# Block-sparse attention and a Fourier mixing layer on one core: head pair 6 without mask matmuls, fewer first transfers, last turn by DMA, a new written order

## Chip, core and metric

The kernel runs on one NeuronCore of a Trainium2 chip. The metric is the device time of one execution in microseconds, as the median of several runs. Five engines work side by side, each through its own instructions in order: PE (TensorE: matmuls and transposes, which write PSUM), DVE (VectorE), ACT (ScalarE), POOL (GpSimd) and SP (SyncE, which here only issues DMA transfers). They wait for each other by semaphores. An engine whose next instruction must wait does nothing else in the meantime.

## What is computed

Attention over 4 batches, 8 heads, 768 positions, head size 64. A query sees the keys of its own block of 64 and of the best blocks out of 12, by the score of the query with each block's mean key, all under the causal mask:

```python
k_rep = k.reshape(B, H, 12, 64, D).mean(axis=3)
gate = where(causal_blocks, einsum('bhsd,bhnd->bhsn', q, k_rep), -1e9)
sel = top 3 of gate for each query, and its own block
scores = where(sel & causal, q @ k.T / sqrt(D), -1e9)
x = softmax(scores) @ v                    # to (4, 768, 512)
X = fft(fft(x, axis=1), axis=2)
u = x + real(X)
un = (u - mean(u)) / sqrt(var(u) + 1e-6)
out = u + relu(un @ w_ch1) @ w_ch2         # 512 -> 2048 -> 512
```

## The kernel before

Work goes by *head pair*: two heads of one batch, 16 pairs in all, pair P in batch P // 4. The order of all work is written out by hand in `ORDER` (L117): a list of some thousand steps such as `s:6,1` (score tile 1 of pair 6). The loop at its end calls one small function for each, and every engine runs its instructions in the order in which they are issued there. The steps that matter here:

- Loads: `Lk`, `Lq`, `Lv` bring a pair's k, q and v in through SP's queue, `LT` and `LF` the two Fourier tables (`fs_sb`, `fd_sb`), `Lc` further constants, among them 0/1 block rows (`ind`) for the score operands; `W:0` to `W:2` bring w_ch1 in three chunks through POOL's queue, for hidden tiles 0-3, 4-9 and 10-15.
- Attention of a pair: `tk`, `tq` turn k and q on PE (six fp32 transposes each, L293). `ks` (DVE, L298) sums k by blocks, `kh` multiplies by a 0/1 table `half` to keep the two heads apart, `qc` (DVE, L317) copies q, `kc` (ACT) and `qs` (POOL) write k and q as fp16 score operands into one of three slots `qk_s`. `g` (PE) is the gate, `gt`, `gx`, `gl`, `gm` (DVE) find the third largest and make a mask of 0 and a large negative number, turned back. `s:P,i` (PE) are the scores of tile i out of 6, `e` (ACT, L432) the exponentials, `d` (POOL, L438) clears what is above the diagonal, `vc` (POOL) casts v, `v` (PE, L450) is the product with v, `x` (DVE) divides.
- Masks come in two forms. Pairs under `NX` = 7 add the mask to the scores by extra matmuls (L422): a block table times the mask, four for each piece of a tile. From pair 7 on, the mask stands as 32 further rows (64 to 95) beside the 64 rows of q, and the block rows beside those of k, so that one matmul with 96 rows does both (L415); step `K` (POOL, L229) writes these rows with 8 copies. In this form each head has a plane of its own in the slot, and q and k are written as two half copies. Pairs of the first form use one plane of a slot, chosen by `XW`.
- Fourier layer of a batch: `fs`, `fd`, `f` (DVE) fold x by symmetry; `y:b,h` (PE, L519) transforms along the features; for the row at the middle frequency, three one-column matmuls (L525) are added twice a batch. `tr` (DVE) and `ty` (ACT) copy it out, `m` (PE, L553, L554) transforms along positions, `u` (DVE, L567) adds x and sums, `xu` (ACT, L579) centres.
- Turn of the centred rows to put the features on partitions: for batches 0 and 3 by PE transposes (`xt`, L586) and a DVE copy (`un`, L591), for batches 1 and 2 by DMA transposes on SP's queue (`un`, L594).
- Hidden layer: `w:b,it` (PE, L630 and L632) makes hidden tile `it` of 16, `r` (ACT L642, every fourth DVE L640) the relu, `c:b,st,h` (PE, L649) multiplies row tile `st` of 6 with w_ch2 over half h of the hidden tiles, `o` (DVE, L655) scales and adds u, `od` (SP, L660) writes out. `bn`, `nv`, `nr` make the variance and its root.

`u` tiles live in five buffers, three a batch, so a later `u` waits until an earlier one was written out. PSUM is handed out as four buffers to every PE product. At the start 12 matmuls on zeros (`warmps`, L677) run while the first k and q arrive; the identity for the transposes (`id32`) and `half` are loaded by DMA on ACT's queue.

Of the kernel before, what the change touches and what calls it, by code (L numbers as in the profile page):

```python
# [20 lines left out]
DM = 512  # L21
# [7 lines left out]
def _consts_np():  # L29
# [36 lines left out]
    for e in range(2):  # L66
        ind[e, 16 * e:16 * e + NB] = nn[:, None] == (s[None, :] // 64)
    half = np.zeros((128, 2, NB), np.float32)
    half[0:64, 0] = 1.0
    half[64:128, 1] = 1.0  # L70
    return dict(FS=fs.astype(np.float16), FD=fd.astype(np.float16),
                ident32=np.eye(128, dtype=np.float32),
# [4 lines left out]
                ind=ind.transpose(1, 0, 2).copy().astype(np.float16),  # L77
                half=half.reshape(128, 24))
# [39 lines left out]
Lk:1 Lq:1 Lk:2 tk:0 tq:0 Lk:3 Lq:2 ks:0 Lq:3 qc:0 tk:1 iz:1 kh:0 qs:0 g:0 ks:1 iz:0 gt:0 kc:0 tq:1  # L118
kh:1 gx:0 kc:1 Lq:4 Lk:4 Lv:0 gl:0,0 tk:2 gl:0,1 gm:0 qc:1 kc:2 s:0,1 s:0,0 ks:2 e:0,1 qs:1 g:1
e:0,0 gt:1 s:0,2 s:0,3 gx:1 e:0,2 tq:2 gl:1,0 tk:3 e:0,3 kh:2 Lq:5 Lv:1 Lk:5 gl:1,1 qc:2 s:0,5  # L120
d:0,3 s:0,4 e:0,5 gm:1 d:0,2 tq:3 ks:3 e:0,4 d:0,5 qs:2 g:2 qc:3 kc:3 d:0,4 s:1,0 gt:2 qs:3 s:1,5
e:1,0 s:1,2 gx:2 tq:4 d:0,0 e:1,5 kh:3 gl:2,0 e:1,2 s:1,1 gl:2,1 s:1,3 qc:4 e:1,1 tk:4 vc:0 gm:2
e:1,3 g:3 ks:4 d:0,1 Lv:2 Lq:6 d:1,5 s:1,4 gt:3 d:1,1 tq:5 e:1,4 d:1,3 gx:3 qs:4 v:0 kc:4 qc:5
d:1,2 d:1,0 d:1,4 s:2,5 x:0 s:2,0 vc:1 e:2,5 s:2,1 e:2,0 s:2,4 d:2,5 Lv:3 Lk:6 Lq:7 LT:0 gl:3,0
v:1 e:2,1 fs:0,0 gl:3,1 kh:4 gm:3 e:2,4 d:2,1 s:2,2 x:1 d:2,0 g:4 vc:2 e:2,2 s:3,2 gt:4 Lv:4 s:2,3
fs:1,0 e:3,2 fs:1,1 tk:5 Lc:0 LF:0 Lq:8 Lk:7 qs:5 gx:4 e:2,3 Lk:8 s:3,4 ks:5 d:3,2 tq:6 d:2,4
e:3,4 fs:0,1 gl:4,0 s:3,1 Lq:9 kh:5 kc:5 gl:4,1 g:5 d:3,4 qc:6 d:2,2 e:3,1 d:2,3 s:3,0 gm:4 vc:3
tk:6 e:3,0 gt:5 d:3,1 s:3,5 Lv:5 Lk:9 ks:6 s:3,3 e:3,5 v:2 e:3,3 d:3,5 gx:5 d:3,0 kh:6 gl:5,0 kc:6
d:3,3 s:4,5 x:2 s:4,2 qs:6 e:4,5 s:4,1 e:4,2 v:3 gl:5,1 fs:2,1 e:4,1 gm:5 d:4,2 fs:2,0 s:5,5 x:3
s:5,4 e:5,5 s:5,1 e:5,4 d:5,5 g:6 fd:2,0 e:5,1 fs:3,0 s:5,2 fs:3,1 s:5,0 fd:2,1 e:5,2 fd:3,1 s:5,3  # L130
fd:3,0 e:5,0 gt:6 s:4,0 f:0,1 s:4,3 e:5,3 f:0,0 s:4,4 gx:6 e:4,0 y:0,0 f:0,3 e:4,3 gl:6,0 f:0,2
e:4,4 gl:6,1 y:0,1 pg:0 tr:0,0 d:5,0 d:4,5 d:4,3 gm:6 tk:7 ty:0,0 d:4,4 tr:0,1 d:5,1 tq:8 d:5,3
vc:4 ks:7 ty:0,1 m:0,2 W:0 qc:8 Lv:6 kc:7 tk:8 d:4,0 u:0,2 d:4,1 tq:7 W:1 kc:8 m:0,0 Lq:10 Lk:10
qc:7 d:5,4 vc:5 m:0,1 u:0,0 xu:0,2 d:5,2 Lv:7 Lq:11 Lk:11 v:4 qs:7 ks:8 xu:0,0 s:6,5 u:0,1 s:6,0
W:2 e:6,5 e:6,0 s:6,3 qs:8 x:4 xt:0,0 xu:0,1 xt:0,2 un:0,0 tq:9 e:6,3 un:0,2 xt:0,1 kh:7 s:6,4
un:0,1 d:6,3 g:7 e:6,4 fs:4,0 w:0,3 fs:4,1 gt:7 d:6,4 gx:7 d:6,5 w:0,0 d:6,0 r:0,3 w:0,6 gl:7,0
r:0,0 gl:7,1 kh:8 gm:7 qc:9 K:7 g:8 r:0,6 w:0,1 gt:8 gx:8 s:6,1 r:0,1 bn:0,0 s:6,2 e:6,1 w:0,11
Li:0 qs:9 bn:0,3 e:6,2 v:5 r:0,11 d:6,1 d:6,2 bn:0,1 s:7,5 tk:9 e:7,5 gl:8,0 x:5 s:7,3 d:7,5 kc:9
vc:6 w:0,10 gl:8,1 Lv:8 Lq:12 Lk:12 gm:8 w:0,5 r:0,10 ks:9 K:8 e:7,3 bn:0,4 s:7,0 tq:10 bn:0,5
e:7,0 v:6 qc:10 r:0,5 vc:7 s:7,4 d:7,0 Lv:9 Lq:13 x:6 d:7,3 s:8,1 e:7,4 tk:10 fs:6,1 e:8,1 s:7,1  # L140
Lk:13 fs:6,0 w:0,2 fd:6,1 e:7,1 fd:6,0 d:8,1 ks:10 s:7,2 r:0,2 X:0 w:0,15 e:7,2 fs:5,1 kh:10 kh:9
# [46 lines left out]
def kernel(  # L188
# [16 lines left out]
    NPAIR = B * NP  # L205
    NSLOT = 3
    NVS = 4
    NX = 7

    C = _consts_np()  # L210
    dr = {n: nc.inline_tensor(C[n], name=f"c_{n}") for n in C}

# [71 lines left out]
    def XW(P):  # L284
        return 1 if P in (0, 1, 2, 6) else 0
# [483 lines left out]
```

## Time and profile before

| | |
|---|---|
| time, median of 3 runs | 303.32 us (302.75 to 303.55) |
| the profiled execution | 303.12 us, of it 301.4 us span from first to last instruction |
| granted TensorE clock, mean | 0.998 |
| PE busy | 289.3 us (96%) |
| DVE busy | 190.5 us (63%) |
| ACT busy | 164.2 us (54%) |
| POOL busy | 111.5 us (37%) |
| DMA | 32.81 MB, mean 109 GB/s |

Busy times are of the whole span, and an average over stages that are limited by different things. PE's matmuls overlap, and their ends are modelled: the mean duration of one (379 ns for 512 columns) is longer than the time from one start to the next, which is what counts for a full PE. The chain view lists the work that set the end, in order of time: start, length, engine, tile written and line, and a count.

### The profile page before, as it was taken

The page shows a single profiled execution, that of the slowest core. Times are in us where ns is not written, and L with a number is a line of the kernel's source. Part 1 is how long each engine was busy: PE and PEld are TensorE (multiplying, and loading weights), DVE is VectorE, ACT ScalarE, POOL GpSimd, SP SyncE. Part 2 cuts the span into 40 slices and gives each one's busy share as a digit, 9 for nine tenths or more (in the row PEclk, how much of TensorE's full clock was granted, in tenths as well). Part 3 has the DMA queues.
Part 4 walks back from the last instruction along what each step waited for, and adds up shares of the span by engine and source line. Part 5 has one row for each costly group of instructions (what it writes and reads, how often), then busy time and mean ns, then how long its engine had stood idle before and what let it go on. Part 6 is the DMA issues. An engine that isn't in the chain of part 4 may idle for free.

```text
span 301.4 us, 6743 instructions
## 1 busy us (share of the span) xinstructions
PE 289.3 (96%) x2644; PEld 178.1 (59%) x2644; DVE 190.5 (63%) x591; ACT 164.2 (54%) x205; POOL 111.5 (37%) x283
## 2 busy tenths in 40 slices
PE   8799989899999999899999999999999999998994
PEld 3476667757766675465667666555666445554441
DVE  1999999998888879599768900936372254321004
ACT  1798999947987748664875696021555010453000
POOL 1266626857685595845572632001100000300000
PEclk9999999999999999999999999999999999999999
DMA  8999997998999867602100003012100010200005
GB/s 195 263 233 229 254 232 160 215 215 204 236 175 212 199 139 106 159 33 75 72 0 2 3 0 67 32 59 90 71 2 0 0 72 35 104 2 0 0 2 209
DMA packets 90079, 32.81 MB, mean 109 GB/s; under 512 B 82816, under 2 KB 86720, under 8 KB 90048
## 3 DMA queue, kind: packets, MB, share of 16 engines
q1 hardware_dynamic: 84096, 27.68, 38.6%
q0 software_dynamic: 3664, 4.19, 8.2%
q10 hardware_dynamic: 2288, 0.51, 0.8%
q8 instruction: 21, 0.34, 0.4%
q14 instruction: 10, 0.08, 0.1%
HBM read 28.71 MB, written 6.29 MB: 116 GB/s over the span
## 4 chain that ended last, share of the span: by engine, by line
PE 86%; DVE 12%; issue 1%; ACT 0%; DVEq 0%
PE c L649 28%; PE h L630 18%; PE h L632 9%; PE sc L415 7%; PE av L450 7%; PE tp L293 4%; PE yp L519 3%; DVE q L317 2%; PE warmps L677 2%; DVE u L567 2%; DVE kr L298 1%; PE sc L410 1%; PE mx L554 1%; PE mx L553 1%; PE g L343 1%; DVE x L226 1%
## 5 line engine op out<-in xcount | busy, mean ns | idle before, releaser
L432 ACT ACTIVATE pt<-sc 128x1024 f16<-128x1024 f32 (+1 forms) x96 | 83.6, 920 | 20.7 <-PE sc L415 17.0
L649 PE MATMUL c<-w_sb,hT 128*128 128x512 f16 x384 | 86.2, 379 | 0.9 <-ACT hT L642 0.9
L630 PE MATMUL h<-unT,w 128*128 128x512 f16 x256 | 84.6, 379 | 0.0
L632 PE MATMUL h<-unT,w 128*128 128x256 f16 x256 | 69.7, 272 | 0.0
L642 ACT ACTIVATE hT<-h 128x768 f16<-128x768 f32 x48 | 38.3, 812 | 44.8 <-PE h L632 44.7
L649 PEld LDWEIGHTS <-hT 128*128 128x128 f16 x384 | 37.0, 98 | 43.2 <-ACT hT L642 1.3
L438 POOL TENSOR_SCALAR_AFFINE_SELECT pt<-pt 128x256 f16<-128x256 f16 x96 | 38.7, 422 | 45.0 <-ACT pt L432 44.1
L630 PEld LDWEIGHTS <-w 128*128 128x128 f16 x256 | 25.0, 98 | 29.0 <-issue 0.7
L655 DVE SCALAR_TENSOR_TENSOR u<-c,rs,u 128x512 f32<-128x512 f32 x24 | 17.5, 746 | 33.4 <-PE c L649 33.4
L579 ACT ACTIVATE x<-u,nm 128x512 f16<-128x512 f32 x24 | 16.0, 717 | 37.9 <-DVE nm L573 37.8
L640 DVE TENSOR_SCALAR hT<-h 128x768 f16<-128x768 f32 x16 | 15.1, 952 | 24.9 <-PE h L632 24.9
L293 PE MATMUL tp<-id,nat 128*128 128x128 f32 x192 | 26.0, 277 | 1.9 <-DVE u L567 1.4
L632 PEld LDWEIGHTS <-w 128*128 128x128 f16 x256 | 25.0, 98 | 3.9
L229 POOL TENSOR_SCALAR_AFFINE_SELECT qk<-mt 32x160 f16<-32x160 f16 x72 | 23.1, 341 | 11.2 <-DVE mt L387 9.7
L415 PE MATMUL sc<-qk 96*128 96x512 f16 (+3 forms) x144 | 26.6, 305 | 0.0
L229 POOL TENSOR_SCALAR_AFFINE_SELECT qk<-q 64x768 f16<-64x768 f32 (+1 forms) x25 | 20.6, 825 | 12.2 <-DVE q L317 11.4
L293 PEld LDWEIGHTS tp<-id,nat 128*128 128x128 f32 x192 | 21.0, 141 | 5.7 <-issue 1.8
L567 DVE SCALAR_TENSOR_TENSOR u<-mx,x 128x512 f32<-128x512 f32 x24 | 15.6, 688 | 13.9 <-PE mx L554 6.2
L226 POOL TENSOR_TENSOR t<-vr,rs 128x6 f32<-128x6 f32 x12 | 2.4, 199 | 56.8 <-DVE rs L610 56.1
L450 PEld LDWEIGHTS <-pt 128*128 128x128 f16 x672 | 22.2, 97 | 1.7 <-issue 0.5
L450 PE MATMUL av<-v,pt 128*128 128x65 f16 x672 | 23.0, 193 | 0.0
L415 PEld LDWEIGHTS <-qk 96*128 96x128 f16 x144 | 13.0, 97 | 8.0 <-issue 0.5
(86 smaller groups left out, 344.7 us busy)
## 6 DMA issues: line engine op xcount, KB each, us to landing
nat<-in_v_dram SPq DMA_DIRECT2D x16, 384.0 KB, 4.4
out_dram<-u SPq DMA_DIRECT2D x24, 256.0 KB, 2.0
nat<-in_k_dram SPq DMA_DIRECT2D x31, 192.0 KB, 4.4
nat<-in_q_dram SPq DMA_DIRECT2D x31, 192.0 KB, 3.7
w_sb<-in_moe_w_ch_dram POOLq DMA_DIRECT2D x2, 1024.0 KB, 12.5
w<-in_moe_w_ch_dram POOLq DMA_DIRECT2D x2, 768.0 KB, 11.1
fs_sb<-c_FS SPq DMA_DIRECT2D x1, 582.0 KB, 5.2
w<-in_moe_w_ch_dram POOLq DMA_DIRECT2D x1, 512.0 KB, 6.8
```

The costliest lines, as they stand in the source:

```text
L229: nc.gpsimd.affine_select(out=out, in_=in_, pattern=[[0, i] for i in n], base=0, channel_multiplier=0, compare_op=ALU.is_ge, fill=0.0)
L293: nc.tensor.transpose(ps[:, 128 * st:128 * st + 128], src[:, st, :], id32)
L415: nc.tensor.matmul(ps[:, e, co:co + q1 - q0], qk[0:96, e, 1, 128 * jt:128 * jt + 128], qk[0:96, e, 0, q0:q1], start=True, stop=True)
L432: nc.scalar.activation(out=d["pt"][:, o:o + 2 * n].rearrange("p (e c) -> p e c", e=2), in_=d["sc", i][:, :, 0:n], func=AF.Exp, scale=0.125)
L438: nc.gpsimd.affine_select(out=dg, in_=dg, pattern=[[0, 2], [1, 128]], base=0, channel_multiplier=-1, compare_op=ALU.is_ge, fill=0.0)
L450: nc.tensor.matmul(av[:, e, 66 * st:66 * st + 65], pt[:, co:co + 128], vv[:, e, jt, 0:65], start=(cnt == 0), stop=(cnt == 20))
L567: nc.vector.scalar_tensor_tensor(out=u_b[:, k2, :].rearrange("p (m two) -> p two m", two=2), in0=mps[:, k2, :].rearrange("p (two m) -> p t ...
L630: nc.tensor.matmul(hp[:, 0:512], w1s, unT[:, dt, 0:512], start=(dt == 0), stop=(dt == NDT - 1))
L632: nc.tensor.matmul(hp[:, 512:768], w1s, unT[:, dt, 512:768], start=(dt == 0), stop=(dt == NDT - 1))
L642: nc.scalar.activation(out=hT, in_=hp, func=AF.Relu)
L649: nc.tensor.matmul(c_ps[b, g[0]][:, st - g[0], :], h_t[b, it][:, 128 * st:128 * (st + 1)], w2_sb[:, it, :], start=(it == 0), stop=(it == N ...
L655: nc.vector.scalar_tensor_tensor(out=o, in0=c_ps[b, g[0]][:, st - g[0], :], scalar=st_t[b][1][:, st:st + 1], in1=o, op0=ALU.mult, op1=ALU.add)
```

## The change

- `NX` is 6: pair 6 takes the second form of mask. Its 32 mask matmuls and 16 score matmuls of 64 rows become 16 of 96 rows, its gate becomes narrower, and a step `K:6` appears. The block rows of slot 0 are loaded with the others in `Lc`; step `Li` is gone. `XW` is 1 for pairs 0 to 2 alone.
- The identity is made on POOL (a memset and two selects), `half` by three DVE memsets; their two transfers are gone. 9 zero matmuls instead of 12. A new tile `mid` is cleared at the start.
- The middle-frequency matmuls take a 128-column weight tile `mid`, of which only column 0 is not zero and is copied in by DVE in step `f:b,1`, and write all 128 rows.
- Batch 3's rows are turned by DMA transposes like those of batches 1 and 2; its steps `xt` are gone.
- Row tile 5 of batch 3 is made in two halves of 256 columns, each over all 16 hidden tiles, with its own `o` and `od` (numbered 5 and 6).
- The order is written anew from the first step to the last.

```diff
-    half = np.zeros((128, 2, NB), np.float32)
-    half[0:64, 0] = 1.0
-    half[64:128, 1] = 1.0
...
-                ident32=np.eye(128, dtype=np.float32),
...
-Lk:1 Lq:1 Lk:2 tk:0 tq:0 Lk:3 Lq:2 ks:0 Lq:3 qc:0 tk:1 iz:1 kh:0 qs:0 g:0 ks:1 iz:0 gt:0 kc:0 tq:1
...
-vc:4 ks:7 ty:0,1 m:0,2 W:0 qc:8 Lv:6 kc:7 tk:8 d:4,0 u:0,2 d:4,1 tq:7 W:1 kc:8 m:0,0 Lq:10 Lk:10
...
-W:2 e:6,5 e:6,0 s:6,3 qs:8 x:4 xt:0,0 xu:0,1 xt:0,2 un:0,0 tq:9 e:6,3 un:0,2 xt:0,1 kh:7 s:6,4
...
-w:3,0 r:3,7 r:3,0 c:3,2,0 c:3,0,0 c:3,3,0 c:3,5,0 c:3,1,0 c:3,4,0 c:3,0,1 c:3,3,1 c:3,2,1 c:3,1,1
...
-o:3,3 od:3,3 c:3,4,1 o:3,0 od:3,0 o:3,1 c:3,5,1 od:3,1 o:3,4 o:3,2 od:3,4 od:3,2 o:3,5 od:3,5
...
+Lq:1 Lk:1 Lq:2 Lk:2 tk:0 Lk:3 ks:0 tq:0 Lq:3 Lv:0 kh:0 qc:0 iz:1 tq:1 qs:0 kc:0 g:0 Lq:4 qc:1 gt:0
+tk:1 qs:1 gx:0 kc:1 gl:0,0 iz:0 tq:2 gl:0,1 gm:0 Lq:5 Lk:4 Lv:1 ks:1 s:0,4 s:0,0 e:0,4 kh:1 qc:2
...
+Lk:6 LT:0 Lq:7 kc:5 gx:4 e:2,1 Lv:4 Lk:7 Lq:8 kh:5 gl:4,0 s:3,5 s:3,3 gl:4,1 e:3,5 x:1 d:2,1 s:3,4
...
+tk:6 f:0,2 e:4,2 f:0,0 y:0,1 f:0,1 e:5,0 ks:6 pg:0 y:0,0 d:5,5 vc:4 tr:0,1 kc:6 d:4,0 Lv:6 Lq:9
...
+d:4,4 m:0,0 kc:7 qs:6 u:0,2 m:0,1 u:0,0 xu:0,2 v:4 W:1 u:0,1 W:2 xu:0,0 xt:0,2 g:6 qs:7 un:0,2
...
+xu:0,1 xt:0,0 gt:6 s:5,2 un:0,0 vc:5 e:5,2 xt:0,1 gx:6 tk:8 Lv:7 un:0,1 d:5,2 tq:8 kc:8 vc:6 x:4
...
+w:0,0 Lv:8 Lk:10 Lq:10 Lq:11 gl:6,0 gl:6,1 w:0,2 r:0,0 kh:7 gm:6 ks:8 K:6 w:0,3 r:0,2 qc:8 g:7
...
+r:0,3 w:0,8 qs:8 bn:0,2 s:6,1 gt:7 r:0,8 w:0,7 gx:7 e:6,1 fs:4,1 s:6,5 gl:7,0 s:6,2 kh:8 e:6,5
...
+xu:3,0 c:2,4,0 un:3,0 m:3,1 c:2,0,1 u:3,1 xu:3,1 bn:3,2 c:2,1,1 un:3,1 c:2,2,0 o:2,1 od:2,1 o:2,0
...
+bn:3,1 od:2,0 c:2,2,1 m:3,2 c:2,5,0 u:3,2 xu:3,2 bn:3,4 c:2,3,0 bn:3,3 un:3,2 bn:3,0 c:2,4,1
...
+c:2,3,1 c:2,5,1 o:2,2 bn:3,5 od:2,2 w:3,12 o:2,4 od:2,4 o:2,5 w:3,0 r:3,12 o:2,3 od:2,5 nv:3
...
+c:3,2,0 r:3,9 c:3,4,0 c:3,5,0 c:3,3,0 c:3,0,0 c:3,4,1 c:3,3,1 o:3,4 od:3,4 c:3,2,1 c:3,1,0 o:3,2
...
+o:3,5 od:3,2 o:3,3 od:3,5 c:3,0,1 od:3,3 c:3,1,1 c:3,5,1 o:3,0 od:3,0 o:3,1 od:3,1 o:3,6 od:3,6
...
-    NX = 7
+    NX = 6
...
+    wid = ctile([128, 128], FP, "wid")
+    mid = ctile([128, NST, 128], F16, "mid")
...
-        return 1 if P in (0, 1, 2, 6) else 0
+        return 1 if P < NSLOT else 0
...
+            nc.vector.tensor_copy(out=mid[:, :, 0:1], in_=zw[:, :, 128:129])
...
-                            nc.tensor.matmul(yps[0:1, gg, o:o + KQ],
-                                             zw[:, 3 * par + s2, 128:129],
+                            nc.tensor.matmul(yps[:, gg, o:o + KQ], mid[:, 3 * par + s2, :],
...
-        if b in (0, B - 1):
+        if b == 0:
...
+        if (b, st) == (B - 1, NST - 1):
+
+            c_ps[b, st + h] = pst([128, 256], f"c{st + h}_{b}")
+            for it in range(NIT):
+                nc.tensor.matmul(c_ps[b, st + h], h_t[b, it][:, 128 * st:128 * (st + 1)],
+                                 w2_sb[:, it, 256 * h:256 * h + 256], start=(it == 0),
+                                 stop=(it == NIT - 1))
+            return
...
+    def w2_rows(b, st):
+        if b == B - 1 and st >= NST - 1:
+            return NST - 1, slice(256 * (st - NST + 1), 256 * (st - NST + 2)), c_ps[b, st]
+        g = next(x for x in (W2_LAST if b == B - 1 else W2_SETS) if st in x)
+        return st, slice(0, DM), c_ps[b, g[0]][:, st - g[0], :]
+
     def w2_o(b, st):
-        g = next(x for x in (W2_LAST if b == B - 1 else W2_SETS) if st in x)
-        o = u_t[b, st // 2][:, st % 2, :]
-        nc.vector.scalar_tensor_tensor(out=o, in0=c_ps[b, g[0]][:, st - g[0], :],
-                                       scalar=st_t[b][1][:, st:st + 1],
+        st, cols, ps = w2_rows(b, st)
+        o = u_t[b, st // 2][:, st % 2, cols]
+        nc.vector.scalar_tensor_tensor(out=o, in0=ps, scalar=st_t[b][1][:, st:st + 1],
                                        in1=o, op0=ALU.mult, op1=ALU.add)
 
     def w2_out(b, st):
-        nc.sync.dma_start(out[b, 128 * st:128 * (st + 1), :], u_t[b, st // 2][:, st % 2, :])
+        st, cols, _ = w2_rows(b, st)
+        nc.sync.dma_start(out[b, 128 * st:128 * (st + 1), cols], u_t[b, st // 2][:, st % 2, cols])
...
-                if who == 1 and e == 0:
-                    nc.scalar.dma_start(id32, dr["ident32"].ap())
+        nc.gpsimd.memset(wid, 1.0)
+        nc.gpsimd.affine_select(out=wid, in_=wid, pattern=[[-1, 128]], base=0, channel_multiplier=1,
+                                compare_op=ALU.is_ge, fill=0.0)
+        nc.gpsimd.affine_select(out=id32, in_=wid, pattern=[[1, 128]], base=0, channel_multiplier=-1,
+                                compare_op=ALU.is_ge, fill=0.0)
         nc.vector.memset(dummy, 1.0)
         nc.scalar.activation(out=dummy, in_=dummy, func=AF.Exp)
         nc.vector.memset(wsrc, 0.0)
         wps = pst([128, 512], "warmps")
-        for _ in range(12):
+        for _ in range(9):
             nc.tensor.matmul(wps, wsrc[:, 0:128], wsrc, start=True, stop=True)
         nc.vector.tensor_copy(out=dummy, in_=wps[:, 0:1])
         nc.vector.tensor_copy(out=id16, in_=id32)
+        nc.vector.memset(half, 0.0)
+        for e in range(2):
+            nc.vector.memset(half[64 * e:64 * e + 64, e, :], 1.0)
         nc.vector.memset(lt, 0.0)
+        nc.vector.memset(mid, 0.0)
         nc.vector.memset(ltb, 0.0)
         for i in range(NSLOT):
             nc.gpsimd.memset(kr_s[i], 0.0)
             nc.gpsimd.memset(kr2_s[i], 0.0)
         for i in range(NVS):
             nc.gpsimd.memset(v_s[i][:, :, :, 64:66], 1.0)
-        nc.scalar.dma_start(half, dr["half"].ap().rearrange("p (e n) -> p e n", e=2))
         nc.scalar.dma_start(indc, dr["indc"].ap())
         nc.scalar.dma_start(lim, dr["lim"].ap().rearrange("p (b n) -> p b n", n=4))
         nc.scalar.dma_start(oth, dr["oth"].ap().rearrange("p (b n) -> p b n", n=NB))
@@ -696,7 +714,7 @@
 
     def consts_next():
         nc.sync.dma_start(oth2, dr["oth2"].ap().rearrange("p (b e n) -> p b e n", e=2, n=16))
-        for i in range(1, NSLOT):
+        for i in range(NSLOT):
             nc.sync.dma_start(qk_s[i][64:96, :, 1, :], dr["ind"].ap())
...
-    def ind_slot0():
-        nc.sync.dma_start(qk_s[0][64:96, :, 1, :], dr["ind"].ap())
```

## The prediction

> **What bounds the kernel now.** I first cut the span in two, at the first hidden-layer matmul (L630, at 61.67 us in the timeline; called the pivot here), and asked for each engine's busy time ahead of it and behind it. The first line names the columns: stretch, length, then busy time and count of each engine, clock, DMA share, GB/s.
>
> ```profile
> core 0: us, PE busy (x) PEld busy (x) DVE busy (x) ACT busy (x) POOL busy (x), PEclk, DMA share, GB/s
> 7.30:61.67 54.37, 49.78 (x778) 36.43 (x776) 52.48 (x175) 48.59 (x61) 30.72 (x58) 1.00 1.03 226
> 61.67:297.69 236.02, 233.57 (x1852) 138.95 (x1848) 136.44 (x411) 114.07 (x143) 79.83 (x211) 1.00 0.34 78
> ```
>
> Ahead of the pivot DVE is busy 52.48 of 54.37 us: DVE sets when the pivot comes. Behind it PE is busy 233.57 of 236.02, and DVE only 136: PE's own work sets the end. The chain of waits in order of time confirms this and shows the few places where it leaves PE (start, length, what):
>
> ```profile
> 1.31 5.30 PE warmps L677 x12
> 6.61 0.67 PE tp L293 x6
> 7.30 0.97 DVE kr L298
> ...
> 101.49 1.62 PE yp L519 x19
> 103.11 0.34 PE yp L525 x3
> 103.46 0.36 PE yp L519 x3
> ...
> 126.72 1.32 DVE u L567 x4
> ...
> 275.82 0.82 ACT hT L642
> 276.68 20.91 PE c L649 x96
> 297.69 0.75 DVE u L655
> ```
>
> Five things are to be seen: DVE can start at 7.30 only, after warm-up and first transposes; three one-column L525 take 113 ns each where a full L519 takes 85; a stop for `u` at 126.72; a stop for the last relu at 275.82; and a tail of 0.75 and what follows. The waits say what the stop for `u` is:
>
> ```profile
> DVE u L567 <- DMA out_dram<-u: 4.5, 2, 2.4
> ```
>
> `u:1,2` waits until an output has left its buffer, and the chain has PE behind it. The shapes and transfers that the change touches:
>
> ```profile
> L336 PE MATMUL g<-q,kr 128*32 128x288 f32 x56 | 4.8, 417 | 1.5 <-DVE kr L226 1.0 <-DVE q L317 0.4
> L343 PE MATMUL g<-q,krb 128*32 128x160 f32 x72 | 4.3, 311 | 0.0
> L586 PE MATMUL xt<-id,x 128*128 128x128 f16 x48 | 3.5, 219 | 0.0
> L519 PEld LDWEIGHTS <-fg 128*128 128x128 f16 x96 | 7.8, 97 | 2.7 <-issue 1.4 <-DVE fg L496 0.2
> ```
> ```profile
> w<-in_moe_w_ch_dram POOLq DMA_DIRECT2D x2, 768.0 KB, 11.1
> unT<-x SPq DMA_TRANSPOSE x12, 2.4
> ```
>
> I count in two ledgers: when the pivot comes (DVE), and what PE does behind it. Durations below are times from one start to the next in the timeline, which are shorter than a group's mean (512 columns: 0.216 us, not 0.379).
>
> **The start.** Nine warm-up matmuls at 0.427 us, from 1.31, end at 5.15 instead of 6.43. Half speed is seen from 0.427 against 0.216. By the row (warm-up of any length, transposes at once at 0.67 for six) `tk:0` would end at 5.82. The Trainium skill speaks against that (TensorE: Matmul & The Clock Gate, Part 1): the slow clock lasts for a time of activity, some 3.4 us in a free-running window, not for a number of matmuls. The trace had 5.2 us of slow work before the clock rose; with the same phase the six transposes run at half speed, 1.31 us, and end at 6.46. DVE is in any case occupied until about 6.5: release at 5.44, the copy of the identity 0.19, `half` 0.1 (three of 0.06), `lt` 0.15, `mid` 0.38 (by columns from 0.272 for 256 and 0.178 for 144), `ltb` 0.15. So `ks:0` starts at 6.5 by the row, 6.7 by the rule; I take 6.7: **-0.6**. The identity on POOL: a memset of about 0.2 and two selects, between the 0.34 of a 32x160 and the 0.83 of a 128x768 one; ready by 2.7 at the latest, while k lands at 4.1 (0.83 + 3.3). The two transfers taken off ACT's queue hid behind the warm-up: 0.
>
> **The order ahead of the pivot.** I listed the DVE steps up to the last `un` of batch 0 in both orders. The new one leaves `ks:8` and `qc:8` (0.87 each), `x:4` (1.14), `kh:7` (0.1), and pair 6's last mask steps `gl`, `gm` (0.41, 0.39) for later; with a few hundredths of the narrower gate, 3.8 us of 51.5. DVE is 97% busy there, so the pivot comes **-3.8** earlier, if the chain x, f, y, tr, m, u, xu, xt, un still has enough DVE work between its links: it has 17 us of DVE work from `x:3` on, of which about 14 are its own, and PE and ACT links of about 4, some of them under the rest. Bounds -1.5 (links bare) to -4.5 (the 1.9 us of idle shrinks); I take -3.8, since both orders show DVE steps of pairs 6 and 7 between the links. The loads must keep up: the DMA share is 1.03 there. q of pair 9 was issued by 43.7, landed 3.7 later and was used at 59.5, so 4.4 us less leave a cover of some 8. Pivot: 61.67 - 0.6 - 3.8 = 57.3.
>
> **Behind the pivot.** *Deferred work:* PE leaves one `tq` (0.65), four score tiles and parts of a gate to after the pivot, 2.87 in all. *Pair 6:* its scores and masks took 2.44 us without waits. The skill (same page, Part 3, The mechanism) has matmuls of few rows run at the same time in different row groups; by that, two heads of 64 rows stream 2688 columns and masks 2176, 4864 in all, against 5376 for 96 rows: the change would lose 0.2. The trace has the switches between the groups too: 2.44 against 5376 x 0.216/512 = 2.28. I take the row: -0.16, and the gate 0.69 to 0.41, -0.28. *Turn of batch 3:* 24 transposes of 0.056, -1.35. Together total PE work falls by 1.8, so behind the pivot it rises by 2.87 - 1.8 = **+1.1**. *Middle frequency:* from 102.87 to 104.27 twelve starts take 1.41 us; at 0.0855 they take 1.03; the rest goes with one-column loads and both switches. L519's own full loads (97 ns) hide, so 0.38 a batch, three behind the pivot: **-1.1** (bounds 0 and -1.5). The DVE copy into `mid`, about 0.08 as the like copies in the folds, is in the DVE sum ahead of the pivot and covered behind it. *Stops:* before the last `c` the relus on which it waits are now of hidden tiles 9, 11 and 15, while its first half reads 0 to 7: **-1.07**. `u:1,2` now waits for outputs issued before four transposes and two row tiles earlier: **-1.56**.
>
> **Covers.** POOL gets 4 us more for pair 6 (8 copies of 0.385; q as two halves of 0.89 for 0.79), ACT 0.85; POOL is busy 30.7 of 54. `K:6` must end before `s:6,1`: `gm:6` ends about 2.1 after the last `un`, K takes 3.1, PE has 3 hidden tiles, a gate and one tile, 5.6: covered by 0.4. *w_ch1 chunks:* POOL issues the second one 6.3 us after the last fold (ten `d` of 0.36, a `vc` 0.86, two q halves 1.74), at about 51.7; it lands 10.8 to 11.1 later, at 62.6; `w:0,8` wants it at 57.3 + 3.9 + 0.4 = 61.6. **+1.0** (bounds 0, as the first chunk is long gone, and 2.6, if the third is as late). What is late next is score tile `s:6,1`, behind it on PE. *DMA transposes of batch 3:* on SP they stand behind outputs of batch 2. From the end of `m:3,2`: `u` 1.5, `xu` 1.3, two transposes of 1.2 and landing 2.4, about 6.2 us; PE has five `c`, 8.6. Covered by 2.4; uncovered it would cost the rest. The three DVE copies gone (0.6 each) were covered. *New small stops* in a new order: 0 to 2, I take **+0.5**.
>
> **The end.** The last `o` handles 256 columns, about 0.41 for 0.75, and its transfer half the bytes: **-0.4** (bounds -0.2, -0.7).
>
> Sum: -4.4 (pivot) + 1.1 - 1.1 - 1.07 - 1.56 + 1.0 + 0.5 - 0.4 = -5.9. The profiled execution, 303.12 with a span of 301.4, becomes 297.2 with 295.5; it lay 0.2 under the median of 303.32, so **297.4**.
>
> **Rivals.**
> - *The pivot hardly moves* (the links of batch 0's chain become the bound; the DVE steps put off were only filling). For it: ahead of the pivot ACT is busy 48.6 and PE 49.8 of 54, not far behind DVE. Against: 97%. Then 3.8 is lost and the 1.0 for w_ch1 with it: 300.2.
> - *PE takes new waits behind the pivot*: both late chunks (2.6), `K:6` not in time (its 3.1 bare), so 5.7 in place of 1.5: 301.6. Against: the first chunk has left POOL's queue long before, and `gm:6` stands only one `x` and the gate's steps behind the pivot on DVE.
> - *Slower*: `LT` now stands behind `Lc` on SP, and `Lc` waits for the last score of pair 2. By DVE sums `Lc` is released at 6.7 + 21.8 + 1 = 29.5, the six issues ahead of `LT` take about 6.7 (2.1 for the first in the trace), landing 5.2: 41.4. `y:0,1` wants the table at about 43.8, a cover of 2.4. It decides from 8.3 us of delay. SP's longest wait for scores was 7.2; two in turn, 14.4, give 297.4 + 12.0 = 309.4.
> - *Better*: no wait for w_ch1, no new stops, all of the middle frequency: 295.5.
>
> **How the numbers follow.** A measurement of this kernel tells about 0.3% (0.9 us) from no change. Chances: forecast 0.55, pivot not moved 0.17, waits behind 0.14, better 0.10, slower 0.04. The range 294.8 to 301.4 holds the forecast, the better case, most of the unmoved pivot and part of the waits. Faster by over 0.3% is under 302.4: 0.93; within: 0.03; slower: 0.04.
>
> **What would show it.** First `kr` (L298) near 6.7; first L630 near 57.3 with DVE as busy ahead of it; no L586 after batch 0; L525's place without gaps; no stops near 126 and before the last `c`; a wait of the fifth hidden tile or of `s:6,1` near 62. Wrong, if DVE idles 4 us or more ahead of the pivot, or if PE idles over 3 us behind it.

## The result, and the profile after

The changed kernel takes 300.58 us (median of 4 runs, 300.15 to 300.79) where the kernel before took 303.16 on the same chip (302.75 to 303.55): a ratio of 0.9913 with a 95% interval of 0.9895 to 0.9931. It is faster by 2.6 us; 5.9 were forecast. The profiled execution took 300.68 with a span of 299.0 us, 2.4 under the 301.4 of before.

The same two stretches as in the prediction, now for the changed kernel: from the first DVE reduction to the first hidden-layer matmul (the pivot, now at 62.24), and from there to the last `o`. The columns are those of the first fence of the prediction.

```profile
6.68:62.24 55.56, 48.57 (x731) 35.61 (x730) 52.89 (x173) 45.70 (x57) 29.84 (x57) 0.97 1.02 222
62.24:295.08 232.84, 232.80 (x1854) 141.90 (x1851) 139.30 (x419) 118.37 (x148) 83.06 (x222) 1.00 0.35 83
```

The second row is what was hoped for, and more: 232.84 us where the kernel before had 236.02, and PE is busy in all but 0.04 of them. The first row is where the gain went. It starts at 6.68 instead of 7.30, as forecast, and yet it is longer than before, 55.56 for 54.37, and its PE clock is 0.97 where it was 1.00. DVE "busy" reads 52.89, which looks like the same full engine as before. The chain of waits in order of time has a new entry in this stretch:

```profile
1.31 4.04 PE warmps L692 x9
6.29 0.38 DVE mid L699
6.76 0.82 DVE kr L296
...
48.57 2.94 issue
51.52 1.01 DVE tr L537
...
277.73 1.75 PE c L647 x16
279.48 13.81 PE c L655 x64
```

The two stops of before, for `u` at 126.72 and for the relu at 275.82, are gone. In their place stand 2.94 us of "issue" at 48.57, time for which the profile shows no releaser, ahead of the transposing copy `tr`. Who waits for that copy is in the waits of the stretch from 45 us to the pivot (us in total, times, longest):

```profile
PEld L551 <- DVE tr L537: 3.2, 1, 3.2
PE mx L551 <- DVE tr L537: 3.0, 1, 3.0
ACT ty L531 <- DVE tr L537: 2.8, 1, 2.8
```

And the timeline around it (start, length, engine and line; in brackets the idle time before) shows what stands ahead of `tr` on DVE:

```profile
47.51 3.27 POOL L436 TENSOR_SCALAR_AFFINE_SELECT pt<-pt 128x256 f16<-128x256 f16 x9
...
47.85 3.74 DVE L221 TENSOR_TENSOR krb<-kr,half 128x24 f32<-128x24 f32 x1
...
50.74 1.70 POOL L224 TENSOR_SCALAR_AFFINE_SELECT qk<-q 64x768 f16<-64x768 f32 x2
...
51.52 1.00 DVE L537 CAST tr<-yp 128x768 f16<-128x768 f32 x1
...
52.57 0.28 PE L551 MATMUL mx<-fd_sb,tr 128*128 128x256 f16 x1 [2.97 <-DVE tr L537]
```

A multiply of 24 elements per partition, `kh:6` in the order, takes 3.74 us; at other places of the same trace it takes 0.18. It starts while POOL runs its diagonal selects `d` one straight behind the other, and ends at 51.59, 0.04 after the first of the two q halves has ended (50.74 + 0.82 = 51.55). POOL's second q half starts at 51.62; the 0.07 us between the two is the first moment since the multiply's start in which POOL runs nothing. DVE is in order, so `tr:0,0` is 3.6 us late, `ty` on ACT and `m:0,2` on PE with it, and PE idles 2.97 us. The busy column counts the blocked multiply as work: from 47.90 to 51.50 DVE is "busy" for 3.60 of 3.60 us with two instructions. And some time after PE's idle stretch its granted clock falls to about half (0.52 in the second row of this view):

```profile
47.90:51.50 3.60, 1.48 (x12) 1.00 (x10) 3.60 (x2) 1.81 (x2) 3.60 (x10) 1.00 0.71 160
53.50:57.00 3.50, 3.48 (x18) 2.40 (x17) 3.43 (x11) 2.82 (x5) 2.94 (x4) 0.52 1.07 204
```

### The profile page after: what moved, and what is told of

Read it like the earlier page. It is cut to its first block, busy times and chain, and to the rows that moved or that the text cites. A ratio compares the mean times of both kernels' runs of the same rounds, so it can differ in the third digit from the quotient of the medians.

```text
span 299.0 us, 6690 instructions
## 1 busy us (share of the span) xinstructions
PE 286.7 (96%) x2601; PEld 180.5 (60%) x2601; DVE 194.0 (65%) x600; ACT 165.7 (55%) x206; POOL 114.6 (38%) x295
## 4 chain that ended last, share of the span: by engine, by line
PE 86%; DVE 9%; issue 2%; ACT 2%; DVEq 0%
PE c L655 27%; PE h L628 19%; PE h L630 9%; PE sc L413 8%; PE av L448 6%; PE tp L291 4%; PE mx L551 2%; PE yp L518 2%; PE mx L552 2%; DVE kr L296 1%; PE g L341 1%; PE warmps L692 1%; PE c L647 1%; ACT pt L430 1%; DVE x L221 1%
## 5 line engine op out<-in xcount | busy, mean ns | idle before, releaser
L655 PE MATMUL c<-w_sb,hT 128*128 128x512 f16 x368 | 83.7, 379 | 0.0
L655 PEld LDWEIGHTS <-hT 128*128 128x128 f16 x368 | 35.4, 98 | 39.3 <-issue 0.5
L436 POOL TENSOR_SCALAR_AFFINE_SELECT pt<-pt 128x256 f16<-128x256 f16 x96 | 37.9, 416 | 54.1 <-ACT pt L430 52.8
L667 DVE SCALAR_TENSOR_TENSOR u<-c,rs,u 128x512 f32<-128x512 f32 (+1 forms) x25 | 17.2, 723 | 28.0 <-PE c L655 27.7
L224 POOL TENSOR_SCALAR_AFFINE_SELECT qk<-mt 32x160 f16<-32x160 f16 x80 | 25.5, 340 | 19.4 <-DVE mt L385 17.8
L413 PE MATMUL sc<-qk 96*128 96x512 f16 (+3 forms) x160 | 28.9, 306 | 0.0
L291 PE MATMUL tp<-id,nat 128*128 128x128 f32 x192 | 26.7, 279 | 1.2 <-DMA nat<-in_q_dram 0.6
L224 POOL TENSOR_SCALAR_AFFINE_SELECT qk<-q 64x768 f16<-64x768 f32 (+1 forms) x26 | 21.4, 824 | 7.7 <-DVE q L315 6.7
L413 PEld LDWEIGHTS <-qk 96*128 96x128 f16 x160 | 14.4, 98 | 9.2 <-issue 0.5
L224 POOL TENSOR_SCALAR_AFFINE_SELECT v<-nat 128x768 f16<-128x768 f32 x16 | 14.5, 908 | 10.5 <-PE av L448 6.9
```

The lines of the kernel that those rows point to most:

```text
L224: nc.gpsimd.affine_select(out=out, in_=in_, pattern=[[0, i] for i in n], base=0, channel_multiplier=0, compare_op=ALU.is_ge, fill=0.0)
L291: nc.tensor.transpose(ps[:, 128 * st:128 * st + 128], src[:, st, :], id32)
L413: nc.tensor.matmul(ps[:, e, co:co + q1 - q0], qk[0:96, e, 1, 128 * jt:128 * jt + 128], qk[0:96, e, 0, q0:q1], start=True, stop=True)
L436: nc.gpsimd.affine_select(out=dg, in_=dg, pattern=[[0, 2], [1, 128]], base=0, channel_multiplier=-1, compare_op=ALU.is_ge, fill=0.0)
L655: nc.tensor.matmul(c_ps[b, g[0]][:, st - g[0], :], h_t[b, it][:, 128 * st:128 * (st + 1)], w2_sb[:, it, :], start=(it == 0), stop=(it == N ...
L667: nc.vector.scalar_tensor_tensor(out=o, in0=ps, scalar=st_t[b][1][:, st:st + 1], in1=o, op0=ALU.mult, op1=ALU.add)
```

## The experiments

**Is it the late multiply that holds the pivot?** In two kernels `kh:6` alone is changed: in the first it stands behind four more DVE steps, where nothing urgent is behind it; in the second it stays in place and has one input instead of two.

```
 # e1_kh_later: ORDER
-... tq:7 kh:6 d:4,3 tr:0,0 ...     ... qs:6 u:0,2 m:0,1 ...
+... tq:7 d:4,3 tr:0,0 ...          ... qs:6 u:0,2 kh:6 m:0,1 ...
 # e2_kh_one_input: a_half(P)
+        if P == NX:
+            for e in range(2):
+                h = slice(64 * e, 64 * e + 64)
+                nc.vector.tensor_reduce(out=kr2_s[P % NSLOT][h, e, 0:NB],
+                                        in_=kr12[h].rearrange("p (n o) -> p n o", o=1),
+                                        axis=mybir.AxisListType.X, op=ALU.add)
+            return
```

> The changed kernel with one DVE step moved: the halving multiply of pair 6 (kh:6, two SBUF inputs) stands behind u:0,2 instead of ahead of tr:0,0. Theory (the multiply is kept out by POOL's ten selects in a row, and everything behind it on DVE, the transposing copy tr:0,0 first, is 3.6 us late; PE then idles 3.1 us and runs the next matmuls at half clock for some 1.6 us): the multiply takes 0.2 to 0.5 us at its new place, the first hidden matmul comes at 57.3 to 58.0 instead of 62.24, the second w_ch1 chunk, issued at the same time as before, is then waited for by 1 to 1.6 us, and the time falls by 3.0 to 4.2 us to 296.4 to 297.6. Rival (the links of batch 0's chain, not this step, set the first hidden matmul): it stays at 61.5 or later and the time within 0.8 us of the changed kernel's 300.6.

> The changed kernel in its own order; kh:6 alone is computed another way at the same place on DVE: two reductions over an axis of one element, 64x12 each, with one SBUF input instead of a multiply with two (the other halves are zero from the start). Theory (it is the second SBUF input that POOL keeps out): the two steps take 0.1 to 0.3 us together although POOL's selects run on, and the time is that of the kernel with kh:6 moved, 296.4 to 297.6. Rival 1 (the step waits for something else at that place, a semaphore or the data): they take or wait 3.5 us as well, 300.6. Rival 2 (any DVE access to SBUF is kept out by POOL): the same.

Measured: 297.27 us for the first (296.83 to 297.31; ratio to before 0.9798, interval 0.9781 to 0.9815) and 297.30 for the second (297.06 to 297.31; 0.9800, 0.9784 to 0.9816). Both are 3.3 us under the changed kernel, and both also beat the kernel before by about 6. DVE's timeline in the first:

```profile
46.49 1.99 DVE L536 CAST tr<-yp 128x768 f16<-128x768 f32 x2
48.36 0.95 DVE L314 COPY q<-tp 128x768 f32<-128x768 f32 x1
...
51.92 0.17 DVE L220 TENSOR_TENSOR krb<-kr,half 128x24 f32<-128x24 f32 x1
```

and in the second, with the multiply's replacement where the multiply had been:

```profile
47.84 0.31 DVE L304 TENSOR_REDUCE krb<-kr 64x12 f32<-64x12 f32 x2
48.18 1.02 DVE L544 CAST tr<-yp 128x768 f16<-128x768 f32 x1
```

The pivot comes at 58.40 and 58.83 instead of 62.24. In the second kernel the step takes 0.31 us in place of 3.74, 3.43 less, and the pivot is 3.41 earlier with the same start (the first kernel started 0.5 us earlier, at 6.17): the whole delay of the step reached the pivot. The half clock behind PE's idle time added little. In the changed kernel DVE waits once for a slow matmul, 0.16 us at 57.25; in the second kernel one small scaling (`nm`, at 55.11) takes 0.54 us where it takes 0.17 in the changed one, so that the two nearly cancel. One part of the expectation was wrong: no w_ch1 chunk was waited for. The stretches of the first kernel:

```profile
6.17:58.40 52.23, 47.19 (x734) 35.18 (x732) 49.72 (x173) 45.74 (x57) 29.80 (x57) 1.00 1.10 238
58.40:291.20 232.80, 232.79 (x1854) 141.86 (x1851) 139.22 (x418) 118.27 (x148) 82.77 (x222) 1.00 0.36 83
```

Behind the pivot there are again 232.80 us, full of PE's work. The second chunk was issued at 51.94, as late as forecast, but landed in 8.3 us where I had taken 10.8 from the row of before.

**What keeps the multiply out?** One POOL instruction that only writes, put in the middle of the burst, tells whether the burst is what it waits for. And two plain copies in place of the multiply tell whether one input is enough to stay clear.

```
 # e3_pool_memset: ORDER, and a new step zz
-... qc:7 d:5,0 d:5,4 ty:0,0 ...
+... qc:7 d:5,0 zz:0 d:5,4 ty:0,0 ...
+        "zz": lambda _: nc.gpsimd.memset(scrap, 0.0),        # scrap: 128x256 float16
 # e4_kh_copy: a_half(P), as in e2_kh_one_input with
+                nc.vector.tensor_copy(out=kr2_s[P % NSLOT][h, e, 0:NB], in_=kr12[h])
```

> The changed kernel with one more POOL instruction: a memset of a scratch tile (128x256, it only writes) between the fourth and the fifth of the eight selects that follow the start of kh:6. Theory (the multiply gets its turn at the first moment when no POOL instruction that reads SBUF is running or queued): the multiply ends within 0.3 us of the end of the fourth or fifth select, about 49.4, and takes some 1.6 us instead of 3.74; the first hidden matmul comes 2 to 4 us earlier. Rival (it waits for the particular select pair of qs:6, or for PE): it still takes 3.7 us or more, as POOL's work is only longer.

> The changed kernel in its own order; kh:6 as two DVE copies of 64x12 float32 from SBUF to SBUF, one input each. If a copy with one input stays clear of POOL the two take 0.1 to 0.3 us and the first hidden matmul comes at 57.3 to 58.0. By the Trainium skill (SBUF, Who interferes with whom) a float32 copy from SBUF to SBUF may run in a mode that uses both port pairs and then is kept out like the multiply: 3.5 us or more, and the first hidden matmul near 62. I expect the second.

DVE and POOL with the memset (298.56 us in its one run):

```profile
47.88 1.52 DVE L221 TENSOR_TENSOR krb<-kr,half 128x24 f32<-128x24 f32 x1
49.32 1.00 DVE L538 CAST tr<-yp 128x768 f16<-128x768 f32 x1
```
```profile
47.53 1.83 POOL L437 TENSOR_SCALAR_AFFINE_SELECT pt<-pt 128x256 f16<-128x256 f16 x5
49.31 0.30 POOL L737 MEMSET scrap<- 128x256 f16 x1
49.57 1.47 POOL L437 TENSOR_SCALAR_AFFINE_SELECT pt<-pt 128x256 f16<-128x256 f16 x4
```

The memset follows the select before it as closely as the selects follow each other (0.35 us from start to start), and yet the multiply now ends at 49.40, between the start of the memset at 49.31 and the next select, and the pivot comes at 60.09: it follows the memset. With two copies (300.89 us in its one run):

```profile
47.62 3.90 DVE L304 COPY krb<-kr 64x12 f32<-64x12 f32 x2
51.56 1.01 DVE L542 CAST tr<-yp 128x768 f16<-128x768 f32 x1
```

The first of the two takes 3.72 us, the second 0.17, and the pivot is at 62.42. The first ends at 51.35, again in a short gap between POOL's two q halves (51.32 to 51.38). So one input is not enough by itself; the reduction stays clear and the copy doesn't. This is what the Trainium skill states (SBUF — State Buffer, Who interferes with whom): DVE and GpSimd share one pair of SBUF ports, held exclusively for an instruction; a DVE instruction takes it with two SBUF inputs (against a GpSimd instruction that reads SBUF), or in a mode that uses both pairs, which a float32 copy can enter and a reduction cannot. All four runs agree with it; that it is the second input, and not something else about a multiply, that lets POOL keep it out is the page's statement, which no run here separates. But a reader who stops at "for an instruction" would expect a wait of at most one select, 0.40 us by these traces; here the wait was nine to ten instructions in a row, because POOL's selects started 0.36 apart and lasted 0.40 each, with the q half close behind, so that one was always running.

**What each local edit is worth behind the pivot.** That stretch repeats to 0.02 us between runs (232.79 to 232.81 in the changed kernel and the first four experiments, measured to the end of PE's last matmul; 235.90 before). So one profiled run is enough to size an edit there. Each of the next three undoes one edit in the kernel with `kh:6` moved.

```
 # e5_pair6_masks: and K:6 taken out of ORDER
-    NX = 6
+    NX = 7
 # e6_turn_pe: and xt:3,0 xt:3,1 xt:3,2 each ahead of its un:3
-        if b == 0:
+        if b in (0, B - 1):
 # e7_mid_columns: and the tile mid, its memset and its copy taken out
-    nc.tensor.matmul(yps[:, gg, o:o + KQ], mid[:, 3 * par + s2, :], ...
+    nc.tensor.matmul(yps[0:1, gg, o:o + KQ], zw[:, 3 * par + s2, 128:129], ...
```

> The kernel with kh:6 moved, and head pair 6 with mask matmuls again (NX = 7, no K:6). By the rows of the prediction: from the first hidden matmul to PE's last one 232.8 us become 232.8 + 0.16 = 233.0, and the gate's 0.28 lies ahead of it. By the Trainium skill's rule of row groups that run at once: 232.8 - 0.2 = 232.6. Time within 0.7 us of 297.3 in both.

> The kernel with kh:6 moved, and batch 3's rows turned by PE again (24 transposes and three DVE copies in place of six DMA transposes). By the row of 0.056 us for a transpose: 232.8 + 1.35 = 234.1 us behind the first hidden matmul, time 298.6. If PE had a wait for the DMA transposes that the trace does not show, less than 1.35.

> The kernel with kh:6 moved, and the middle frequency as one-column matmuls again, without the tile and the copy for it. By the starts in the trace of before (twelve in 1.41 against 1.03 us): three batches behind the first hidden matmul, 232.8 + 1.1 = 233.9 us; time 298.3. If the switch of shape is hidden: 232.8.

The stretch from the pivot to PE's last matmul in the three, in this order:

```profile
58.67:291.87 233.20, 233.20 (x1886) 141.74 (x1883) 139.65 (x418) 118.56 (x148) 80.69 (x214) 1.00 0.36 84
```
```profile
58.91:293.06 234.15, 234.15 (x1878) 143.17 (x1875) 141.34 (x421) 118.32 (x148) 83.45 (x222) 1.00 0.34 80
```
```profile
58.91:292.89 233.98, 233.98 (x1854) 141.02 (x1851) 138.24 (x415) 118.33 (x148) 82.92 (x222) 1.00 0.36 84
```

Against 232.80 the turn of batch 3 is worth 1.35 us (forecast 1.35), the middle frequency 1.18 (forecast 1.1), and pair 6 0.40 where 0.16 was forecast. The single times are 297.81, 298.39 and 298.56.

For pair 6 the estimate from the skill's rule (TensorE: Matmul & The Clock Gate, Part 3, The mechanism), a loss of 0.2, has the wrong sign, but the rule itself, that matmuls of few rows run at the same time in different row groups, is seen in the trace of before:

```profile
66.97 0.27 PE L632 MATMUL h<-unT,w 128*128 128x256 f16 x1
67.08 0.38 PE L630 MATMUL h<-unT,w 128*128 128x512 f16 x1
67.29 0.27 PE L632 MATMUL h<-unT,w 128*128 128x256 f16 x1
67.50 0.39 PE L410 MATMUL sc<-qk 64*128 64x256 f16 x4
...
67.92 0.38 PE L410 MATMUL sc<-qk 64*128 64x512 f16 x2
68.14 0.35 PE L422 MATMUL sc<-mt,indz 64*128 64x224 f16 x4
```

The two heads' score matmuls of 512 columns take 0.22 us together (67.92 to 68.14), the time of one. What the estimate lacks is the price of the switches. The hidden-layer matmul of 256 columns ahead of pair 6's scores takes 0.21 us from start to start (67.29 to 67.50), where the one before took 0.11 (66.97 to 67.08). In the run with mask matmuls PE goes three times into this form and three times out of it behind the pivot, and each time costs 0.09 to 0.10 us more: 0.57 in all, less the 0.2 about 0.37 of the measured 0.40. My row of 2.44 us held only the switches out of the form; those into it fall on the matmul ahead, three times 0.096.

The turn has a cost at the end, too: from the end of PE's last matmul to the end of the span the kernel with PE's turn takes 3.31 us and the one with DMA transposes 3.94. By SP's wait for it the last output lands 2.3 us after the last matmul in both. What follows on SP, its other waits and the program's close, takes 1.03 and 1.65. That it comes with the six DMA transposes is shown; why was not tried.

**The start.** Seven warm-up matmuls instead of nine, and DVE's wait for them moved behind its memsets.

```
 # e8_start
-        for _ in range(9):
+        for _ in range(7):
-        nc.vector.tensor_copy(out=dummy, in_=wps[:, 0:1])
         nc.vector.tensor_copy(out=id16, in_=id32)
 ...
         nc.vector.memset(ltb, 0.0)
+        nc.vector.tensor_copy(out=dummy, in_=wps[:, 0:1])
```

> The kernel with kh:6 moved, seven warm-up matmuls instead of nine, and the DVE copy that waits for them put behind DVE's first memsets. If the transposes of k follow the warm-up directly, at half clock: the first reduction (ks:0) at 1.31 + 7 x 0.427 + 1.31 + 0.1 = 5.7 us instead of 6.2 to 6.7, the time 0.4 to 1.0 us lower, 296.3 to 296.9. Rival (the landing of k, or the slow clock that stays longer by as much, sets it): the first reduction at 6.2 or later and no gain.

297.01 us (296.90 to 297.20; ratio 0.9817, interval 0.9790 to 0.9844), which can't be told from the 297.27 without it. The first reduction came at 6.03, between the 5.7 of the theory and the 6.2 of the rival. The second half of k landed at 4.39; the transposes of k began at 4.48 instead of 4.28 (0.63 us after the start of the last warm-up matmul, where one takes 0.43) and ran at half speed, 0.213 us apart for 0.109. DVE waited for them 1.28 us. So the landing of k took about 0.2 of the 0.33 us that were missed, and the rest lies in the transposes. The pivot stayed at 58.53, within what the kernel without this edit gave: the rival is right that nothing is gained.

**What the order is worth, and what the edits are worth without it.** First all local edits in the order of before; I had to place pair 6's new step, and put `K:6` right behind `gm:6`. Then the same without pair 6's edit.

```
 # e9_old_order: the changed kernel with the ORDER of before, in which
-... gm:6 tk:7 ...          ... od:3,2 o:3,5 od:3,5
+... gm:6 K:6 tk:7 ...      ... od:3,2 o:3,5 o:3,6 od:3,5 od:3,6
-Li:0 xt:3,0 xt:3,1 xt:3,2  (at their places)
 # e11_old_order_masks: the same order without K:6, and
-    NX = 6
+    NX = 7
```

> The local edits of the change (start, pair 6, middle frequency, batch 3's turn by DMA, last row tile in two halves) in the order of before; the new order alone is undone. By what the other runs and the prediction give for the edits: start -0.6, pair 6 -0.5, middle -1.1 behind the first hidden matmul and up to -0.4 ahead of it, turn of batch 3 -1.35 plus 0.6 at the end, last halves -0.5; so 303.2 - 3.2 to 303.2 - 4.2, 299.0 to 300.0. Then the new order with its late kh:6 is worth nothing or costs up to 1.6 us against the changed kernel's 300.6, and the order with kh:6 moved (297.3) is worth 1.7 to 2.7. Rival (the order carries the gain, the local edits hide): 302.5 or more.

> The local edits in the order of before again, but with pair 6 by mask matmuls as before; start, middle frequency, turn of batch 3 and last halves stay changed. Theory (in the old order pair 6's edit gives POOL 3.6 us more, which puts its w_ch1 transfers 3.2 us later and keeps DVE's small steps out, and that eats what the other edits save): the w_ch1 transfers start at 50.5 to 51.5 us again, no wait for them, 233.4 us behind the first hidden matmul, 54.5 from the first reduction to it, time 300.0 to 300.8. Rival (the other edits are hidden in the old order): 302.5 or more.

All edits in the old order: 303.88 us (ratio 1.0023, interval 0.9998 to 1.0049), no gain at all: the number is the rival's, not the theory's. Its reason is not, though. Without pair 6's edit the time is 300.72 (0.9896, 0.9868 to 0.9925), so the other edits are not hidden in the old order; pair 6's edit eats them. By the medians it costs 3.2 us in the old order with K's step where I put it (3.9 by the two ratios, as the runs were on different chips and the first kernel's twelve times spread from 302.63 to 305.89), and in the new one it is worth 0.40 behind the pivot. In the old order its price shows at the transfers that POOL issues: with it, the three w_ch1 transfers are issued at 54.1, 55.8 and 59.8 us; without it, at 50.0, 51.7 and 56.3. Behind the pivot the first has 235.61 us and the second 232.80. The waits of the first between 60 and 75 us include

```profile
PE h L628 <- DMA w<-in_moe_w_ch_dram: 1.8, 2, 1.5
```

(in total, times, longest). These 1.8 us are most of the difference of 2.8; another 0.8 is a longer wait of PE for `u` near 127 to 129 us (1.3 for 0.5). Which of pair 6's steps on POOL puts the transfers off was not tried.

The median of the second lies in the forecast range of 300.0 to 300.8, but its four runs fall in two groups, 299.77 and 300.07, and 301.36 and 301.38, and the profiled one is of the longer pair. It had 232.80 us behind the pivot and not 233.4, and 55.53 ahead of it and not 54.5. One DVE step accounts for more than that 1.0, and it looks like the same trap with another instruction, a scaling of two elements per partition:

```profile
52.15 1.59 DVE L571 TENSOR_SCALAR nm<-sm 128x2 f32<-128x2 f32 x1
```

beside this on POOL:

```profile
51.67 0.76 POOL L722 DMA_DIRECT2D w<-in_moe_w_ch_dram  x1
52.45 0.42 POOL L436 TENSOR_SCALAR_AFFINE_SELECT pt<-pt 128x256 f16<-128x256 f16 x1
52.81 0.91 POOL L224 TENSOR_SCALAR_AFFINE_SELECT v<-nat 128x768 f16<-128x768 f32 x1
```

It ends at 53.74, 0.02 after the second select; it takes 0.17 where nothing holds it. When it starts, POOL is issuing a transfer, so what holds it until the first select begins at 52.45 is not a select; that was not tested, nor whether the two shorter runs were spared this wait.

**Two tries for more.** In the kernel with `kh:6` moved, one has PE's transposes of pair 4's q one score tile earlier, where DVE idles 0.55 us; the other takes the small scaling `nm` from DVE to ACT.

```
 # e10_tq_earlier: ORDER
-... d:0,3 s:1,1 e:1,4 d:1,2 tq:4 gl:2,0 ...
+... d:0,3 tq:4 s:1,1 e:1,4 d:1,2 gl:2,0 ...
 # e12_nm_act: m_u
-        nc.vector.tensor_scalar(out=nm, in0=sm[:, 2 * kp:2 * kp + 2],
-                                scalar1=-0.0625 / DM, scalar2=None, op0=ALU.mult)
+        nc.scalar.activation(out=nm, in_=sm[:, 2 * kp:2 * kp + 2], func=AF.Identity,
+                             scale=-0.0625 / DM)
```

> The kernel with kh:6 moved, and the transposes of pair 4's q (tq:4) one score tile earlier on PE, because DVE idles 0.55 us ahead of their copy at 21.1 us. If DVE sets the first hidden matmul here: it comes 0.3 to 0.6 us earlier, 57.8 to 58.1 with the same start, and the time is 296.6 to 297.0. Rival (the exponentials or a later wait take it back): no change, 297.2 or more.

> The kernel with kh:6 moved, and the small step behind each u (nm, 128x2, a scaling from SBUF to SBUF, 12 in all) taken from DVE to ACT, which reads its result anyway; on DVE these three ahead of the first hidden matmul take 0.88 us, of which POOL's selects hold them for about 0.37. Theory (DVE sets the first hidden matmul, and every step of DVE that POOL can keep out is a risk): from the first reduction to the first hidden matmul 51.6 to 52.0 us instead of 52.2, the 232.8 behind it unchanged, the time 296.8 to 297.1. Rival (ACT, with 0.2 us more between u and xu, is now the late link): 297.3 to 297.8.

Both missed, and both times fall where the rival put them: 297.27 (0.9793, 0.9766 to 0.9821) and 297.76 (0.9833, 0.9808 to 0.9857). From the first reduction to the pivot they took 52.49 and 52.88 us, against 52.22. In the first the 0.55 us of idle time is gone, and DVE idles 0.50 at 23.20 instead, for the product with v. In the second `nm` stands on ACT between the `xu` activations; ACT runs six activations of 0.71 each from 53.87 to 57.74 with one `nm` among them, and 232.71 us behind the pivot did not make up for it. So the kernels with `kh:6` moved or made a reduction, at 297.3, are what this study has to offer beyond the change.

## Why the prediction was wrong, point by point

- **The order ahead of the pivot**, "the pivot comes **-3.8** earlier": this is the step that failed. The pivot came at 62.24, 0.57 later than before and 4.9 us behind the forecast 57.3. The condition that I attached ("if the chain ... still has enough DVE work between its links") named the wrong danger. I gave every DVE step its usual duration whatever ran on POOL at that moment. The burst was in my own working ("ten `d` of 0.36, a `vc` 0.86, two q halves 1.74") but only as a delay of POOL's transfers. Its effect on DVE is 3.4 us, by the run with the reduction.
- **What remains of that step**, 1.5 us (pivot 58.83 in that run against 57.3, with the same start): DVE's busy time up to the last `un` of batch 0 fell by 2.86 (52.36 to 49.50), not by 3.8. Of the difference, 0.19 are three memsets of pair 6's gate and 0.17 the copy into `mid` (I had 0.08); about 0.6 net is small two-input or scaling steps that are longer in the new order (`sd` 0.40 a step for 0.36, the minimum with `lim` 0.35 for 0.28, `nm` 0.30 for 0.24; the multiplies of `kr` 0.3 less), which fits more meetings with POOL's selects, but was not followed step by step. DVE idles 0.47 more, and from the end of the last `un` to the pivot it is 0.30 us for 0.13. That sums to 1.6, as near as the rounded 57.3 allows.
- **The start**, -0.6: the number was right, 6.68 for a forecast 6.7, but not by the path that gave it, so it was partly luck. I had let the transposes of k set it, at full speed (the row, 5.82) or at half (the rule, 6.46). They came to an end at about 6.3, as their spacing went from 0.213 to 0.11 us at about 5.8, and DVE was not waiting for them: the chain goes through its own memset of `mid`, which ends at 6.67. I had DVE free at about 6.5; the three memsets of `half` took 0.4 with the gaps between them where I had 0.1. In other runs of the same start the reduction came at 6.17 to 6.68.
- **Behind the pivot**, where the terms of the sum make -1.1: 236.02 became 232.84, so -3.2. The middle frequency and batch 3's turn had the right size, both stops went, pair 6's matmuls gave 0.24 more than the row said, by the switches that it left out (and 5376 columns at 0.216 us for 512 are 2.27 us, not 2.28). The two terms of loss, +1.0 for the second w_ch1 chunk and +0.5 for new stops, did not appear: PE is busy in 232.80 of 232.84 us. These are 1.8 of the 2.1 us; the rest I did not trace. For the chunk the landing time was mis-sized in this order, 8.3 or 9.4 us for 10.8 to 11.1. In the changed kernel that loss could hardly show: the chunk landed at 61.81, ahead of the late pivot. In the two kernels with the pivot at 58.40 and 58.83 it landed at 60.27 and 61.77, without a wait either.
- **The covers**: `K:6` ended in time for `s:6,1` (1.3 us ahead of it in the kernel with `kh:6` moved), and the DMA transposes of batch 3 cost PE nothing.
- **The end**, -0.4: the step itself was right, the last output lands 2.3 us after the last matmul instead of 2.9. SP's close of the program took 0.7 us longer, and the tail grew by 0.1 instead.
- **The rivals**: the measured time is near that of "the pivot hardly moves" (300.2), but its mechanism, bare links of batch 0's chain, is refuted: with one step out of POOL's way and the order otherwise the same, the stretch from the first reduction to the pivot became 3.3 to 3.4 us shorter. "Wrong, if DVE idles 4 us or more ahead of the pivot" was the wrong sign to look for. By the profile DVE idles only 2.67 of the 55.56 us and not at all in the 3.6 us that were lost; it was held, and the held instruction is shown as busy.

The local edits and the order can't be added up one by one either. In the old order all edits together gave nothing, the same without pair 6 gave about 3 us, and in the new order pair 6's edit is a gain.

## What to carry to other kernels

When a change moves work, lay POOL's instructions beside DVE's in the timeline, not only each engine's sum: a DVE step with two SBUF inputs, or a small float32 copy or scaling from SBUF to SBUF, can be held for a whole run of POOL selects, here 3.6 us for a step of 0.18. Look in the trace for instructions far longer than others of their shape; the busy share hides them. The mend is cheap: put the step where POOL does something else and nothing urgent stands behind it, or give it a form that stays clear of POOL (here a reduction over one element).

## What the runs showed of the hardware that was not expected

- POOL's selects in a row never let the held DVE step in between two of them: 3.74 us over ten instructions, 1.52 with one memset after the fourth to follow its start. A gap of 0.07 us on POOL was enough to let it in.
- PE's first matmul starts at 1.31 us in every run, but its speed rose at very different times, told by the spacing of the matmuls (the profile's clock column reads 1.00 throughout): at about 4.2 us in the kernel with `kh:6` moved (512 columns 0.427, then 0.217), and not before 7 in the one with POOL's memset (transposes 0.213, then 0.109). In the first the warm-up ended sooner and released DVE at 4.87 instead of 5.37; the first reduction followed 1.3 us later in both, at 6.17 and 6.68, behind DVE's memsets. PE's timeline in the two, over the warm-up and the first transposes:

```profile
1.31 3.52 PE L691 MATMUL warmps<-zeros 128*128 128x512 f16 x9 [1.31 <-DVE zeros L688]
4.66 0.82 PE L290 MATMUL tp<-id,nat 128*128 128x128 f32 x6
```
```profile
1.31 4.02 PE L693 MATMUL warmps<-zeros 128*128 128x512 f16 x9 [1.31 <-DVE zeros L690]
5.12 2.59 PE L292 MATMUL tp<-id,nat 128*128 128x128 f32 x13
```

- PE's clock also fell late: PE idled from 49.60 to 52.57 in the changed kernel, ran eight matmuls 0.11 to 0.12 us from start to start, and only from about 53.6 to 57.0 took 0.213 (256 columns each).
